# Layer 1: the products of a turned g with wphi issued one unit later, behind the next unit's turn

## The chip, the core and the metric

The kernel runs on one core of one Trainium2 chip. The metric is device time in microseconds of one execution; times are the median of several runs. TensorE (PE) does matmuls and transposes, VectorE (DVE), ScalarE (ACT) and GpSimd (POOL) do elementwise work, and SyncE (SP) issues nearly all DMAs.

## The reference, cut to what matters

A decaying causal attention over 4 batches, 8 heads and 576 positions is followed by a dense layer with a gated activation and by a soft mixture of 8 experts with 4 slots each:

```python
x = attention(q, k, v, f)                       # 2304 tokens x 512
h = x @ w_in                                    # 512 -> 2048
g = h * (1.0 / (1.0 + np.exp(-1.702 * h)))
x2 = g @ w_out                                  # 2048 -> 512
logits = x2 @ phi                               # 512 -> 32 slots
d = softmax(logits, axis=0); slot_in = d.T @ x2
slot_out[e] = np.maximum(slot_in[e] @ w1[e], 0.0) @ w2[e]
out = softmax(logits, axis=1) @ slot_out
```

Here `attention` and `softmax` stand for the reference's own lines, which are unchanged by what follows.

## The kernel before, in words

**What layer 1 computes.** The kernel never forms x2. It folds w_out and phi into one matrix, `wphi = w_out @ phi` (`fold_phi`, lines 240 to 257), so that the logits are `g @ wphi`, and it sums the slots' inputs in the space of g before it goes through w_out once at the end.

**How the work is tiled.** The 2304 tokens are 18 blocks of 128, taken two at a time: 9 chunks c = 0 to 8. A chunk has 8 units (t, fg): block t of two, quarter fg of the 2048 columns. `moe_steps` (lines 765 to 799) makes a unit: twelve fp16 matmuls into one PSUM bank `hp` (lines 775 to 777, four values of k times three products of high and low parts), then ScalarE's tanh (line 788) and VectorE's multiply (line 789) into `g`. The unit is put into the deque `turns`.

**The turn.** `turn(c, t, fg)` (line 731) is called at the end of a later unit; one unit as a rule stays in the deque. TensorE transposes g's four 128x128 pieces into a bank `gT` (line 744, f32), ScalarE copies the bank to `gt` in SBUF (line 751), and TensorE multiplies the four pieces by wphi into `p4` (line 753; the profile calls it p, and shows two records for each of the four f32 matmuls). The four products land in four groups of 32 partitions.

**What follows the last product of a chunk.** When all units of a chunk have been turned, `turn` runs off what is left of the steps of the chunk before and starts `slot_steps` (line 815): VectorE scales p4 into `l4` (line 820), TensorE sums it to logits `lg` in both orientations (lines 828 and 831), VectorE and ScalarE take running maximum and exponentials (lines 841 to 862), TensorE transposes the weights (`d`, line 871) and adds g up by slot (`sp`, line 896), and VectorE merges that into `spart` (line 903). These steps are a generator: each yield of `moe_steps` moves it by one. In the last chunk the two blocks have their own `p4` and their own slot steps.

**Attention beside it.** `attn_items` gives attention's pieces a place and a cost, and the main loop emits as many of them at each yield as a cumulative cost allows. Attention's last transposes of x (line 656) end in the seventh or eighth chunk. Then its pool is closed, and the loads of the expert weights (`load_e`, lines 1026, 1028 and 1031; 256 KB each, 127 of them) go through the SP queue into a ring of tiles: first new ones in the space that attention leaves, then `xt`, `g`, `w`, `gt` and other tiles as these come free. After layer 1 the experts' matmuls (lines 1147, 1169 and 1182) consume them.

**What sets the order.** The program is traced in the order of these calls, and when it is built a scheduler with a simulated timeline puts each engine's instructions in an order: on TensorE, work that the simulation holds ready can pass work that was traced earlier. `tc.issue_after(ins)` ties TensorE instructions of a block to places behind `ins`; no wait on a semaphore comes of it. On the chip each engine takes its instructions in that fixed order.

**Buffers that matter here.** PSUM: `sc` three banks, `mm` three (hp, gT, d, sp), `pv` one, `mi` one. `p4` and `lg` share the single `mi` bank. SBUF: `gt` has three buffers (`N_GT`), shared with the fold's transposed w_out in the first chunks; `g` has seven, of which a chunk takes four.

Of the kernel before, what the change touches and what calls it, by code (L numbers as in the profile page):

```python
# [30 lines left out]
def attention_moe_softmoe(ctx, tc, q, k, v, f, w_in, w_out, phi, w1, w2, out):  # L31
# [17 lines left out]
    NCH = NBLK // 2  # L49
# [11 lines left out]
    def ps_sc(name):  # L61
        return ps.tile([128, 512], F32, tag="sc", name=name, bufs=3)

    def ps_mm(name):
        return ps.tile([128, 512], F32, tag="mm", name=name, bufs=3)
# [4 lines left out]
    def ps_mi(name):  # L70
        return ps.tile([128, 512], F32, tag="mi", name=name, bufs=1)
# [646 lines left out]

    G = {}
    P4 = {}  # L720
    last_turn, last_hp = [None], [None]
    turns, turned, slot, sums = deque(), {}, [iter(())], {}
    N_UNIT = 2 * FG
# [2 lines left out]
    def units(c):  # L726
        if c == 0:
            return [(t, fg) for fg in range(FG) for t in range(2)]
        return [(t, fg) for t in range(2) for fg in range(FG)]

    def turn(c, t, fg):


        one = c == NCH - 1
        first = units(c)[0] if not one else (t, 0)
        if (t, fg) == first:
            P4[c, t if one else 0] = ps_mi("p4")
        p4 = P4[c, t if one else 0][:, 0 if one else 128 * t:][:, 0:128]
        g = G[c, t, fg]
        pt = pt2 = ps_mm("gT")  # L740
        if (c, t, fg) == (NCH - 1, 1, FG - 1):
            pt2 = ps_sc("gT")
        for a in range(4):
            last_turn[0] = nc.tensor.transpose((pt if a < 2 else pt2)[:, a * 128:(a + 1) * 128], g[:, a * 128:(a + 1) * 128], ident)  # L744
        gt = mp.tile([128, 512], F32, tag="gt", name="gt", bufs=N_GT)
        if (c, t, fg) == (NCH - 1, 1, FG - 1):
            nc.scalar.copy(out=gt[:, halves[0]], in_=pt[:, halves[0]])
            nc.vector.tensor_copy(gt[:, halves[1]], pt2[:, halves[1]])
            warm(2)
        else:  # L750
            nc.scalar.copy(out=gt, in_=pt)  # L751
        for a in range(4):
            nc.tensor.matmul(  # L753
                p4[NS * a:NS * (a + 1)], lhsT=wphi[:, 4 * fg + a, :], rhs=gt[:, a * 128:(a + 1) * 128],
                start=((t, fg) == first), stop=(fg == FG - 1), skip_group_check=True,
            )
        turned[c, t] = turned.get((c, t), 0) + 1
        ts = (t,) if one else (0, 1)
        if all(turned.get((c, i), 0) == FG for i in ts):
            for _ in slot[0]:  # L760
                pass
            slot[0] = slot_steps(c, ts)
            next(slot[0])

    def moe_steps(c):
        xt = XT[c]
        for u, (t, fg) in enumerate(units(c)):
# [5 lines left out]
            for kk in range(KD):  # L773
                with tc.issue_after(last_turn[0].ins) if final and kk == KD - 1 else nullcontext():
                    nc.tensor.matmul(hp, lhsT=xt[:, 0, kk, ts], rhs=win(0, fg, kk), start=(kk == 0), stop=False)  # L775
                    nc.tensor.matmul(hp, lhsT=xt[:, 0, kk, ts], rhs=win(1, fg, kk), start=False, stop=False)  # L776
                    last_hp[0] = nc.tensor.matmul(  # L777
                        hp, lhsT=xt[:, 1, kk, ts], rhs=win(0, fg, kk), start=False, stop=(kk == KD - 1)
                    )
                if kk == 1:  # L780
                    if final:
                        while turns:
                            turn(*turns.popleft())
                    yield
# [6 lines left out]
            for _ in range(min(3 if c < 2 else 2, len(turns) - 1)):  # L791
                if turns[0][2] >= folded[0]:
                    break
                turn(*turns.popleft())
# [7 lines left out]
    def warm(k):  # L802

        if not k:
            return
        if not idle:
            idle.append(ps_pv("z").rearrange("p (k n) -> p k n", k=4))
        for _ in range(k):
            tc.keep_in_program_order(
                nc.tensor.matmul(  # L810
                    idle[0], lhsT=ident16, rhs=ident16.unsqueeze(1).to_broadcast([128, 4, 128]), start=True, stop=True
                )
            )

    def slot_steps(c, ts=(0, 1)):
# [4 lines left out]
        nc.vector.tensor_scalar(  # L820
            out=l4, in0=P4.pop((c, ts[0]))[:, 0:128 * nt], scalar1=1.0 / (GS * WS), scalar2=None, op0=ALU.mult
        )
# [216 lines left out]
    if True:  # L1039
# [63 lines left out]
        while turns:  # L1103
            turn(*turns.popleft())
# [72 lines left out]
        for p, (c0, c1) in enumerate(PARTS):  # L1177
# [13 lines left out]
            p4 = (ps_mm if 1 else ps_mi)("p4")[:, 0:w]  # L1191
# [70 lines left out]
```

## Time and profile before

| | |
|---|---|
| median of 3 runs | 575.36 us (575.34 to 577.53) |
| the profiled execution | 572.58 us |
| its span, first to last instruction | 570.9 us |
| TensorE busy | 510.8 us, 89% of the span |
| VectorE, ScalarE, GpSimd busy | 353.3, 309.6, 69.0 us |
| mean granted TensorE clock | 0.97 |
| line 744, transposes of g (288) | 44.5 us, 278 ns each |
| line 751, copies of gT (71) | 40.8 us, 582 ns each |
| line 753, products with wphi (576 records) | 31.1 us, 286 ns each |
| lines 775 to 777, hp (864) | 332.3 us |

All rows are of the one profiled execution, on core 0. Times are microseconds from the start of the span. A row of the timeline gives the start, the duration, engine, source line, operation, and the tiles written and read; xN means that N like instructions were merged. A bracket at its end is the time that the engine stood idle before it and the instruction that ended the wait. Matmuls are pipelined, so the records of neighbours overlap and the distance of their starts says what one costs. A row of waits gives the total, the number of waits and the longest. DMA share is the mean busy share of the 16 DMA engines; their records can overlap, so it can come out above 1.

### The profile page before, as it was taken

To read this page: it belongs to the slowest core of one execution; us is meant where nothing else is said; L and a number is where in the kernel's file an instruction comes from. 1 tells how busy PE (TensorE), PEld (TensorE's weight loads), DVE (VectorE), ACT (ScalarE), POOL (GpSimd) and SP (SyncE) were. 2 spreads that over 40 slices of the span, in tenths; PEclk is the share of its full clock that TensorE was granted. 3 is DMA by queue.
4 is the path that set the end of the run, shared out by engine and by line. 5 is a ranking of instruction groups with operands and counts; after the bars stand their busy time and mean duration, and the time that the engine had idled before them with its cause. 6 is when DMAs were issued, how large, how long until landed. Compare 5 with 4: busy or idle time off the path is not lost.

```text
span 570.9 us, 13573 instructions
## 1 busy us (share of the span) xinstructions
PE 510.8 (89%) x5355; PEld 328.1 (57%) x5355; DVE 353.3 (62%) x934; ACT 309.6 (54%) x596; POOL 69.0 (12%) x120
## 2 busy tenths in 40 slices
PE   4476999999899989989999998988999999999991
PEld 4364877777666556655665664655566554454441
DVE  8978969476755676757685766867565323343032
ACT  5767686666765665646675565665565133312111
POOL 4766643220000000000000000000000000000000
PEclk9969799999999999999999998998999999999997
DMA  9997673978952869997648889986553189999998
GB/s 241 270 355 168 167 126 134 206 183 163 165 95 43 150 101 132 167 180 126 125 87 159 134 158 175 200 139 91 81 94 72 24 276 357 372 388 358 378 302 262
DMA packets 229823, 105.63 MB, mean 185 GB/s; under 512 B 202592, under 2 KB 211296, under 8 KB 229760
## 3 DMA queue, kind: packets, MB, share of 16 engines
q1 hardware_dynamic: 228528, 103.59, 77.9%
q10 hardware_dynamic: 1232, 1.18, 0.7%
q8 instruction: 42, 0.69, 0.5%
q14 instruction: 21, 0.17, 0.1%
HBM read 64.63 MB, written 4.72 MB: 121 GB/s over the span
## 4 chain that ended last, share of the span: by engine, by line
PE 62%; DMA 17%; DVE 9%; ACT 5%; issue 3%; SPq 2%; POOL 0%; DVEq 0%; ACTq 0%; POOLq 0%
PE hp L775 9%; PE hp L777 8%; PE hp L776 8%; DMA ph<-pn 6%; PE gT L744 5%; DMA we<-in_moe_w_dram 4%; PE p L753 4%; PE pv L607 3%; PE sp L896 3%; DMA kf<-in_k_dram 2%; PE pv L612 2%; DMA qf<-in_q_dram 2%; PE scs L536 2%; PE scs L535 2%; DVE low L213 1%
## 5 line engine op out<-in xcount | busy, mean ns | idle before, releaser
L775 PE MATMUL hp<-w,xt 128*128 128x512 f16 x288 | 111.0, 385 | 0.8 <-DVE spart L903 0.8
L776 PE MATMUL hp<-w,xt 128*128 128x512 f16 x288 | 110.7, 384 | 0.0
L777 PE MATMUL hp<-w,xt 128*128 128x512 f16 x288 | 110.6, 384 | 0.0
L562 ACT ACTIVATE pf<-scs,mx 128x512 f32<-128x512 f32 (+3 forms) x108 | 58.3, 543 | 40.7 <-DVE mx L558 30.4
L788 ACT ACTIVATE g<-hp 128x512 f32<-128x512 f32 x72 | 42.6, 592 | 53.0 <-PE hp L777 52.9
L571 DVE SCALAR_TENSOR_TENSOR pn<-pf,pn 128x512 f16<-128x512 f32 (+2 forms) x78 | 51.0, 657 | 32.1 <-ACT pn L570 31.6
L789 DVE SCALAR_TENSOR_TENSOR g<-g,hp 128x512 f32<-128x512 f32 x72 | 49.2, 683 | 34.6 <-ACT g L788 34.4
L570 ACT ACTIVATE pn<-pf 128x512 f16<-128x512 f32 (+2 forms) x78 | 46.9, 604 | 23.4 <-DMA ph<-pn 22.3
L558 DVE CUSTOM_DVE_ANT_0 scs<-scs,zmq 128x256 f32<-128x256 f32 (+3 forms) x96 | 46.9, 497 | 11.8 <-PE scs L536 6.8
L612 PE MATMUL pv<-vv,ph 128*128 128x65 f16 (+2 forms) x360 | 46.7, 198 | 3.5 <-DMA ph<-pn 3.4
L751 ACT COPY gt<-gT 128x512 f32<-128x512 f32 x71 | 40.8, 582 | 14.3 <-PE gT L744 13.5
L777 PEld LDWEIGHTS <-xt 128*128 128x128 f16 x288 | 28.5, 99 | 34.7 <-issue 2.8
L613 PE MATMUL pv<-vv,ph 128*128 128x65 f16 (+2 forms) x360 | 46.1, 196 | 0.0
L614 PE MATMUL pv<-vv,ph 128*128 128x65 f16 (+2 forms) x360 | 45.4, 194 | 0.0
L744 PE MATMUL gT<-ident,g 128*128 128x128 f32 x288 | 44.5, 278 | 1.0 <-DVE g L789 1.0
L775 PEld LDWEIGHTS <-xt 128*128 128x128 f16 x288 | 29.0, 101 | 25.7 <-issue 3.5
L612 PEld LDWEIGHTS <-ph 128*128 128x128 f16 (+2 forms) x360 | 34.5, 101 | 14.6 <-issue 5.8
L776 PEld LDWEIGHTS <-xt 128*128 128x128 f16 x288 | 28.5, 99 | 24.0 <-issue 2.3
L744 PEld LDWEIGHTS gT<-ident,g 128*128 128x128 f32 x288 | 33.3, 142 | 14.2 <-issue 5.1
L535 PE MATMUL scs<-kab,qa 128*128 128x128 f16 x240 | 35.4, 219 | 4.4 <-ACT pf L562 2.5
L613 PEld LDWEIGHTS <-ph 128*128 128x128 f16 (+2 forms) x360 | 34.9, 103 | 2.7 <-issue 0.4
L614 PEld LDWEIGHTS <-ph 128*128 128x128 f16 (+2 forms) x360 | 35.0, 103 | 0.7 <-issue 0.6
(223 smaller groups left out, 1013.4 us busy)
## 6 DMA issues: line engine op xcount, KB each, us to landing
we<-in_moe_w_dram SPq DMA_DIRECT2D x127, 256.0 KB, 5.4
raw<-in_moe_w_in_dram SPq DMA_DIRECT2D x16, 512.0 KB, 7.6
raw<-in_moe_w_out_dram SPq DMA_DIRECT2D x16, 512.0 KB, 6.0
kf<-in_k_dram SPq DMA_DIRECT2D x13, 256.0 KB, 3.7
qf<-in_q_dram SPq DMA_DIRECT2D x13, 256.0 KB, 4.4
vf<-in_v_dram SPq DMA_DIRECT2D x12, 256.0 KB, 4.5
out_dram<-ob SPq DMA_DIRECT2D x12, 256.0 KB, 3.2
ph<-pn SPq DMA_TRANSPOSE x78, 3.3
```

Of the source, the lines that this page charges most:

```text
L558: nc.vector.tensor_tensor_reduce(out=o, in0=o, in1=mask, scale=-SC, scalar=3.0e38 if n == 128 else DG[r][1][:, u], op0=ALU.add, op1=ALU.mi ...
L562: nc.scalar.activation(out=pf[:, hh * nb:(hh + 1) * nb], in_=o, func=AF.Exp, bias=mx[:, hh:hh + 1], scale=-1.0)
L570: nc.scalar.activation(out=pn[:, 0, 0:w], in_=pf, func=AF.Copy, scale=PB)
L571: nc.vector.scalar_tensor_tensor(out=pn[:, 1, 0:w], in0=pf, scalar=PB, in1=pn[:, 0, 0:w], op0=ALU.mult, op1=ALU.subtract)
L612: nc.tensor.matmul(o, lhsT=ph[0:rr, 0, off:off + n], rhs=vh, start=(j == 0), stop=False)
L613: nc.tensor.matmul(o, lhsT=ph[0:rr, 0, off:off + n], rhs=vl, start=False, stop=False)
L614: nc.tensor.matmul(o, lhsT=ph[0:rr, 1, off:off + n], rhs=vh, start=False, stop=(j == i))
L744: last_turn[0] = nc.tensor.transpose((pt if a < 2 else pt2)[:, a * 128:(a + 1) * 128], g[:, a * 128:(a + 1) * 128], ident)
L775: nc.tensor.matmul(hp, lhsT=xt[:, 0, kk, ts], rhs=win(0, fg, kk), start=(kk == 0), stop=False)
L776: nc.tensor.matmul(hp, lhsT=xt[:, 0, kk, ts], rhs=win(1, fg, kk), start=False, stop=False)
L777: last_hp[0] = nc.tensor.matmul(hp, lhsT=xt[:, 1, kk, ts], rhs=win(0, fg, kk), start=False, stop=(kk == KD - 1))
L789: nc.vector.scalar_tensor_tensor(out=g, in0=g, scalar=1.0, in1=hp, op0=ALU.add, op1=ALU.mult)
```

## The change

`turn` keeps the transposes and the copy. The four products, with the allocation of `p4` and the start of the slot steps that follows the last of them, become a function of their own, `by_phi`. A turn first runs `by_phi` for the unit held from the turn before, inside `tc.issue_after` of its own last transpose, and then puts its own unit into `held`. In the last chunk a unit isn't held: its products are issued at once, as before. The start of `slot_steps` for a chunk thus comes in the first turn of the next chunk.

```diff
+    held = deque()
...
     def turn(c, t, fg):
-        one = c == NCH - 1
-        first = units(c)[0] if not one else (t, 0)
-        if (t, fg) == first:
-            P4[c, t if one else 0] = ps_mi("p4")
-        p4 = P4[c, t if one else 0][:, 0 if one else 128 * t:][:, 0:128]
         g = G[c, t, fg]
         pt = pt2 = ps_mm("gT")
...
             nc.scalar.copy(out=gt, in_=pt)
+        with tc.issue_after(last_turn[0].ins):
+            while held:
+                by_phi(*held.popleft())
+        held.append((c, t, fg, gt))
+        if c == NCH - 1:
+            by_phi(*held.popleft())
+
+    def by_phi(c, t, fg, gt):
+        one = c == NCH - 1
+        first = units(c)[0] if not one else (t, 0)
+        if (t, fg) == first:
+            P4[c, t if one else 0] = ps_mi("p4")
+        p4 = P4[c, t if one else 0][:, 0 if one else 128 * t:][:, 0:128]
         for a in range(4):
             nc.tensor.matmul(
                 p4[NS * a:NS * (a + 1)], lhsT=wphi[:, 4 * fg + a, :], rhs=gt[:, a * 128:(a + 1) * 128],
```

What stands behind the products in `turn` (the count of turned units and the start of `slot_steps`) stands behind them in `by_phi` as well.

## Rows read from the trace of the kernel before

**Rows 1.** Windows of core 0: engine busy us (instructions), granted clock, DMA share, GB/s.

```profile
165.00:457.00 292.00, 278.33 (x3085) 172.22 (x3086) 192.17 (x556) 169.40 (x340) 3.56 (x30) 0.99 0.70 120
...
457.00:550.00 93.00, 89.42 (x857) 43.44 (x855) 25.45 (x85) 22.89 (x47) 0.68 (x1) 1.00 1.01 356
```

**Rows 2.** Waits of PE in 165 to 457: us in total, times, longest.

```profile
PE p L753 <- ACT gt L751: 3.4, 4, 2.1
```

**Rows 3.** Timeline of PE: start, us, instruction, [idle before <-releaser].

```profile
113.84 0.43 PE L753 MATMUL p<-gt,wphi 128*32 128x128 f32 x8 [0.71 <-ACT gt L751]
...
334.69 0.43 PE L753 MATMUL p<-gt,wphi 128*32 128x128 f32 x8 [0.94 <-ACT gt L751]
...
335.84 0.60 PE L744 MATMUL gT<-ident,g 128*128 128x128 f32 x4
...
380.93 0.42 PE L753 MATMUL p<-gt,wphi 128*32 128x128 f32 x8 [2.12 <-ACT gt L751]
...
383.89 0.19 PE L612 MATMUL pv<-vv,ph 128*128 128x65 f16 x1
```

**Rows 4.** Timeline of ACT, same columns, 378 to 381.

```profile
378.40 0.63 ACT L302 ACTIVATE kbn<-kf 64x512 f16<-64x512 f32 x1 [2.56 <-DMA kf<-in_k_dram]
...
380.31 0.56 ACT L751 COPY gt<-gT 128x512 f32<-128x512 f32 x1
```

**Rows 5.** Timeline of DVE, same columns.

```profile
334.38 0.68 DVE L789 SCALAR_TENSOR_TENSOR g<-g,hp 128x512 f32<-128x512 f32 x1
...
381.35 0.41 DVE L626 TENSOR_TENSOR x<-pv,rd 128x256 f32<-128x256 f32 x1
```

**Rows 6.** Waits of the SP queue in 440 to 460.

```profile
SPq L1026 <- DVE x L626: 9.5, 1, 9.5
...
SPq L1026 <- PE xT L656: 3.9, 1, 3.9
```

**Rows 7.** Timeline of PE, 457 to 466.

```profile
457.42 0.38 PE L656 MATMUL xT<-ident,x 128*128 128x128 f32 x2
...
460.96 0.38 PE L777 MATMUL hp<-w,xt 128*128 128x512 f16 x1
...
461.18 0.60 PE L744 MATMUL gT<-ident,g 128*128 128x128 f32 x4
...
461.70 0.42 PE L753 MATMUL p<-gt,wphi 128*32 128x128 f32 x8
...
462.06 0.39 PE L775 MATMUL hp<-w,xt 128*128 128x512 f16 x1
...
464.45 0.38 PE L777 MATMUL hp<-w,xt 128*128 128x512 f16 x1
...
464.76 0.42 PE L753 MATMUL p<-gt,wphi 128*32 128x128 f32 x8
...
465.11 0.66 PE L744 MATMUL gT<-ident,g 128*128 128x128 f32 x4
...
465.61 0.38 PE L775 MATMUL hp<-w,xt 128*128 128x512 f16 x1
```

**Rows 8.** Chain that ended last, in order of time, after 515.

```profile
524.94 5.42 DMA we<-in_moe_w_dram
```

**Rows 9.** Timeline of PE: the first and the last of nine.

```profile
169.72 0.43 PE L753 MATMUL p<-gt,wphi 128*32 128x128 f32 x8
...
433.08 0.43 PE L753 MATMUL p<-gt,wphi 128*32 128x128 f32 x8
```

**Rows 10.** Timeline of PE, 478 to 485.

```profile
478.80 0.59 PE L828 MATMUL lg<-l,rsum 128*128 128x256 f32 x2
...
481.50 0.30 PE L871 MATMUL d<-ident,dT 32*128 32x32 f32 x2 [1.27 <-ACT dT L860]
...
484.43 0.64 PE L753 MATMUL p<-gt,wphi 128*32 128x128 f32 x16
```

**Rows 11.** Timeline of DVE, 464 to 512.

```profile
481.74 0.22 DVE L841 TENSOR_TENSOR ee<-lg,rm 128x64 f32<-128x64 f32 x1
```

## The prediction

> **What bounds the kernel now.** I first read the windows of two stretches [rows 1]. From 165 to 457 us, where attention and layer 1 run interleaved, TensorE is busy 278.33 of 292.00 us at a granted clock of 0.99 while the DMA share is 0.70: TensorE sets the pace, and it stands still for 292.00 - 278.33 = 13.7 us. After 457 the picture turns: the DMA share is 1.01 at 356 GB/s, because the expert weights stream in. The chain of waits ends in these loads [rows 8]. The first of them waited for the end of attention: the SP queue stood 9.5 us for the last x and 3.9 us for its transposes [rows 6], which came at 457.42 [rows 7]. So a microsecond that TensorE loses before 457 delays the weight stream and, with it, the end; a microsecond gained inside the stream, between 457 and 510, is worth little.
>
> Next I read TensorE's waits of the first stretch. The wait that the change addresses, products (p) for the copied transpose (gt), is 3.4 us in 4 instances [rows 2]. The timeline shows where [rows 3]: 0.94 us at 334.69, 2.12 us at 380.93, two small ones between 165 and 457 making up the rest, and 0.71 us at 113.84, ahead of that stretch. The largest one's cause stands on ScalarE: it waited 2.56 us for the DMA of a k row, and the gt copy stood behind that row's casts until 380.31 [rows 4].
>
> What the order of TensorE looks like now matters as much. The products don't follow their own transposes even today: in [rows 7] the p at 464.76 belongs to the unit whose transposes ran at 461.18, and stands just ahead of the next unit's transposes at 465.11, a whole unit late. The change mostly moves a group of products from just before the next turn to just behind it.
>
> **The change part by part.** No instruction is added or removed: each of 72 units keeps four transposes, one copy (two in the last unit), and eight product records (p x8, 0.43 us). No DMA is issued by what moves; SP and POOL are passed by nothing.
>
> The stalls. With products held one turn longer, gt has been copied long before. Bounds: nothing, if each stall returns at the next instruction; the full 3.4 us of [rows 2] plus the 0.71 us of [rows 3] at the other end. I follow the two large ones. Without the 0.94 us, TensorE would reach its next transposes at 335.84 - 0.94 = 334.90 [rows 3], and their g is ready at 334.38 + 0.68 = 335.06 [rows 5]: 0.16 us returns. Without the 2.12 us, twelve hp matmuls follow that need nothing of ScalarE's late work; the attention products behind them need the bank that x frees at 381.35 + 0.41 = 381.76 [rows 5], and would come at 383.89 - 2.12 = 381.77 [rows 3]: nothing returns. So I take 3.4 - 0.16 = 3.2 us, and leave out the 0.71 us because before 165 weight loads and conversions share the path.
>
> The order on TensorE. Where p runs directly ahead of the transposes, hp to hp takes from 464.45 to 465.61 = 1.16 us; where transposes run ahead of p, from 460.96 to 462.06 = 1.10 us [rows 7]. The difference, 0.06 us, is what a group saves when it changes sides. Nine groups before 457 stand directly ahead of a whole turn [rows 9]: 9 x 0.06 = 0.5 us. The other groups have other work between, and I take nothing for them. The Trainium skill's page TensorE: Matmul & The Clock Gate (Step-by-step: what each phase is for) speaks against this term: weight loads are pulled ahead of matmuls in flight, so a change of sides should cost and save nothing. By it the sum would be 3.2 us instead of 3.7; here the row decides, since p starts 464.76 - 464.45 = 0.31 us after the last hp and the transposes 461.18 - 460.96 = 0.22 us.
>
> The logits chain. The last products of a chunk now come behind the first turn of the next chunk, so the copy l, both lg matmuls, the softmax and the slot sums (sp) start one unit later. Their lengths stay; the next chunk's first products move by a unit too, so the distance between them is kept. I take nothing. Bounds: below nothing, one group of products (0.43 us) slips past 457.42 and out of the path; above, a wait of 1.27 us like the one in [rows 10] at each of the seven chunk ends before 457, 8.9 us.
>
> Buffers. gt has three, and a held one plus the one being filled makes two. The g tiles of chunk 7 are freed by their sp a unit later, and the weight loads for those slots wait for that; the stream is then already full [rows 1], so I take nothing. In the last chunk nothing is held, so the tail stays.
>
> Sum: 3.2 + 0.5 = 3.7 us less. The profiled execution took 572.58 us (span 570.9), giving 568.9; it lies 2.78 us under the median of 575.36. On the median: 575.4 - 3.7 = 571.7 us.
>
> **Rivals.** *The waits only move (575).* ScalarE was late at 380 because a DMA was late [rows 4], and everything queued behind that cast was late with it. If what runs in the place of the products needs exp, cast or g, TensorE stands one instruction further on. The Trainium skill's page PSUM — Partial Sum Buffer (Engine vs sequencer instructions) says as much: ScalarE's queue is strictly first in, first out. For it: 10.3 of the 13.7 us idle have other causes, and the build-time scheduler places the whole stretch anew. Against it: twelve independent matmuls follow the largest stall. Only the order's 0.5 us would be left: 574.9.
>
> *The single p/lg bank stalls TensorE (580).* p and lg share one PSUM buffer. The next chunk's first products need every reader of lg done: lg starts at 478.80 [rows 10] and its last DVE reader ends at 481.74 + 0.22 = 481.96 [rows 11], 3.16 us later. Today TensorE fills that time with hp, and the first products of the last chunk run at 484.43, two units together [rows 10]. If products tied to a turn stand at TensorE's head earlier than 3.16 us after lg, it stands still. At 1.27 us a chunk end, seven ends give 8.9 us: 575.4 - 3.7 + 8.9 = 580.6. Against it: turns are 465.11 - 461.18 = 3.93 us apart even without attention [rows 7], over 3.16, and the tie orders products behind the turn without forbidding other work between.
>
> *The end of attention moves further (568).* The last x transposes at 457.42 stand behind twelve hp matmuls, and the loads waited 3.9 us for them [rows 6]. A new order that puts them ahead would start the stream up to 3.9 us sooner on top: 571.7 - 3.9 = 567.8. Nothing in the change forces it.
>
> *It does little, because the products are late already* [rows 7]; that ends where the first rival does, and is counted with it.
>
> **How the numbers follow.** About 0.5%, 2.9 us, is what a measurement of this kernel can tell from no change. Forecast 571.7, own range 569.5 to 573.5: 0.42. Waits only move, or little changes, 573 to 577: 0.33. Bank stall, 580.6: 0.17. Attention's end, 567.8: 0.08. Faster than 572.5 takes the two fast cases without the slow end of the forecast, to which I give 0.04: 0.42 - 0.04 + 0.08 = 0.46. Slower than 578.2 is the bank stall, 0.17; within 0.5% remains 0.37. The range 567 to 579 reaches down to the moved end of attention and leaves out the bank stall beyond 579, some 0.15, and 0.03 below.
>
> **What would show it.** The wait of p for gt should be gone from TensorE's waits, or below 0.5 us. TensorE's idle time between 165 us and the last x transposes should fall from 13.7 to about 10.5, and the first weight load should follow the last x transposes, 3 to 4 us sooner. Each group of products should stand right behind a turn, with hp to hp at 1.10 us. If the idle time is unchanged and other waits (ph, qa, lg) have appeared, the first rival holds. If p waits for a reader of lg, or the wait of d for dT grows at the chunk ends, the bank does. I am wrong altogether if the weight stream starts sooner and the end doesn't follow.

## The result and the profile after

The changed kernel took 568.45 us in the median of six runs (563.65 to 571.55) beside 575.35 us (574.63 to 577.53, six runs) before: a ratio of 0.9852 [0.9809, 0.9896] as recorded, 1.5% faster; the two medians alone give 0.988. Two repeats against new runs of before gave 0.989 [0.9847, 0.9933] and 0.9845 [0.98, 0.9891]. The profiled execution took 571.55 us (span 569.8), the longest of its six; those of the repeats took 565.27 and 561.29 us, so where it matters I read all three.

The windows of the kernel after, split where its first weight load starts (454 instead of 457); columns as in [rows 1]:

```profile
165.00:454.00 289.00, 277.34 (x3066) 169.01 (x3066) 191.82 (x554) 168.59 (x340) 3.57 (x30) 0.99 0.73 122
454.00:550.00 96.00, 92.87 (x881) 44.18 (x883) 26.12 (x86) 22.18 (x47) 0.68 (x1) 1.00 0.99 348
```

TensorE stands still for 289.00 - 277.34 = 11.7 us where it was 13.7, and the stage ends 3 us sooner. For a measure that doesn't hang on where a stage ends, I use one fixed window, 165 to 440, in every kernel: before

```profile
165.00:440.00 275.00, 261.33 (x2915) 162.44 (x2916) 184.94 (x533) 164.38 (x329) 3.56 (x30) 0.99 0.74 126
```

and after

```profile
165.00:440.00 275.00, 263.34 (x2925) 160.30 (x2925) 185.83 (x533) 165.56 (x332) 3.57 (x30) 0.99 0.76 127
```

Idle there is 13.7 us before and 11.7 after; a second profile of before gives 14.3, the two repeats of after 10.0 and 8.4.

What TensorE waited for, kernel before, 165 to 457, beside the line of [rows 2]:

```profile
PE pv L612 <- DMA ph<-pn: 3.2, 2, 2.8
PE lg L828 <- DVE l L820: 2.3, 1, 2.3
PE scs L535 <- DMA qa<-qan: 1.9, 1, 1.9
...
PE hp L775 <- DVE spart L903: 0.8, 1, 0.8
PE d L871 <- ACT dT L860: 0.8, 1, 0.8
```

The same view of the kernel after, 165 to 454:

```profile
PE pv L612 <- DMA ph<-pn: 7.5, 7, 2.7
PE gT L740 <- DVE g L798: 1.3, 2, 0.8
PE hp L784 <- ACT gt L747: 1.0, 1, 1.0
PE lg L837 <- DVE l L829: 0.6, 1, 0.6
```

Two things happened, and only one was in my forecast. The wait of p for gt is gone, but 1.0 us came back as a wait of hp (for the copy gt; hp and gT share three banks), and the wait for ph, the DMA that brings attention's probabilities, rose from 3.2 to 7.5 us (6.1 and 5.1 in the repeats). The other: three waits of the chain at the chunk's end, lg for l, d for dT and hp for spart, 2.3 + 0.8 + 0.8 = 3.9 us before, are down to 0.6 us (0.2 and 0.7 in the repeats). I had these rows before me and put them under "other causes".

The largest of them shows how it goes. Before, on TensorE's timeline:

```profile
251.14 0.70 PE L828 MATMUL lg<-l,rsum 128*128 128x256 f32 x2 [2.33 <-DVE l L820]
```

and on VectorE's:

```profile
250.59 0.19 DVE L307 COPY kan<-cpart 128x24 f16<-128x24 f16 x1 [2.59 <-DMA kab<-kan]
250.67 0.42 DVE L820 TENSOR_SCALAR l<-p 128x256 f32<-128x256 f32 x1
```

VectorE stood 2.59 us in front of a copy for attention that waited for a DMA; l was behind it in the queue, and lg was at TensorE's head, waiting for l. The same place after, on TensorE

```profile
250.64 0.38 PE L786 MATMUL hp<-w,xt 128*128 128x512 f16 x1
...
251.66 0.70 PE L837 MATMUL lg<-l,rsum 128*128 128x256 f32 x2 [0.65 <-DVE l L829]
```

and on VectorE:

```profile
250.51 0.19 DVE L307 COPY kan<-cpart 128x24 f16<-128x24 f16 x1 [2.99 <-DMA kab<-kan]
...
251.19 0.42 DVE L829 TENSOR_SCALAR l<-p 128x256 f32<-128x256 f32 x1
```

The DMA is as late (2.99 us) and l comes even later, at 251.19; but TensorE has hp matmuls of the next unit to run, the last of them from 250.64 to 251.02, and lg waits 0.65 us. The delay stayed, the work in front of it grew.

The order from the last x transposes on (timeline of TensorE, after) answers to [rows 7]:

```profile
454.37 0.38 PE L656 MATMUL xT<-ident,x 128*128 128x128 f32 x2
454.68 1.92 PE L905 MATMUL sp<-g,dd 128*32 128x512 f32 x16
...
459.87 0.38 PE L786 MATMUL hp<-w,xt 128*128 128x512 f16 x1
460.08 0.60 PE L740 MATMUL gT<-ident,g 128*128 128x128 f32 x4
460.61 0.43 PE L762 MATMUL p<-gt,wphi 128*32 128x128 f32 x8
460.97 0.39 PE L784 MATMUL hp<-w,xt 128*128 128x512 f16 x1
```

Products stand behind the turn, 460.97 - 459.87 = 1.10 us from hp to hp, as forecast. And chunk 6's slot sums (sp, 1.92 us) now stand behind the last x transposes; before, they ran ahead of them:

```profile
450.26 1.92 PE L896 MATMUL sp<-g,dd 128*32 128x512 f32 x16
```

My bound for what could slip out of the path there was 0.43 us.

The SP queue's wait at the end of attention, as in [rows 6], kernel after:

```profile
SPq L1035 <- PE xT L656: 3.4, 1, 3.4
```

and its longest one from 495 to 515:

```profile
SPq L1037 <- PE sw L938: 5.2, 2, 4.8
```

The first is nearly what it was (3.9): the transposes still stand behind twelve hp matmuls. The second, 5.2 us in two waits, was 2.7 us in two before (495 to 520); while SP waits, the stream thins out. The window of 510 to 515, before:

```profile
510.00:515.00 5.00, 5.00 (x82) 2.54 (x70) 4.04 (x12) 0.41 (x2) 0.68 (x1) 1.00 1.03 362
```

and after:

```profile
510.00:515.00 5.00, 5.00 (x91) 3.32 (x94) 3.52 (x11) 1.23 (x2) 0.68 (x1) 1.00 0.49 157
```

From the first weight load (457.8 before, 454.8 after) to the end of the span it takes 570.9 - 457.8 = 113.1 us before and 569.8 - 454.8 = 115.0 after: some 2 us of the gain are given back there, 1.4 us in the means of two profiles before and three after.

### The profile page after: what moved, and what is told of

It reads as the page before. It is cut to its first block, busy times and chain, and to the rows that moved or that the text cites. A ratio compares the mean times of both kernels' runs of the same rounds, so it can differ in the third digit from the quotient of the medians.

```text
span 569.8 us, 13581 instructions
## 1 busy us (share of the span) xinstructions
PE 512.9 (90%) x5355; PEld 325.7 (57%) x5355; DVE 353.0 (62%) x934; ACT 308.1 (54%) x596; POOL 68.8 (12%) x120
## 5 line engine op out<-in xcount | busy, mean ns | idle before, releaser
L797 ACT ACTIVATE g<-hp 128x512 f32<-128x512 f32 x72 | 42.5, 590 | 47.6 <-PE hp L786 42.6
L612 PE MATMUL pv<-vv,ph 128*128 128x65 f16 (+2 forms) x360 | 45.8, 198 | 8.4 <-DMA ph<-pn 7.5
L558 DVE CUSTOM_DVE_ANT_0 scs<-scs,zmq 128x128 f32<-128x128 f32 (+3 forms) x96 | 46.8, 497 | 10.2 <-PE scs L536 5.5
L740 PE MATMUL gT<-ident,g 128*128 128x128 f32 x288 | 45.2, 279 | 1.7 <-DVE g L798 1.3
L612 PEld LDWEIGHTS <-ph 128*128 128x128 f16 (+2 forms) x360 | 34.3, 101 | 19.0 <-DMA ph<-pn 10.0
L613 PE MATMUL pv<-vv,ph 128*128 128x65 f16 (+2 forms) x360 | 45.0, 195 | 0.0
L614 PE MATMUL pv<-vv,ph 128*128 128x65 f16 (+2 forms) x360 | 44.6, 194 | 0.0
L613 PEld LDWEIGHTS <-ph 128*128 128x128 f16 (+2 forms) x360 | 34.5, 102 | 2.2 <-issue 0.4
L569 POOL MEMSET pn<- 128x128 f16 x12 | 2.5, 206 | 272.3 <-DMA ph<-pn 268.7
```

What stands on the lines that cost most here:

```text
L558: nc.vector.tensor_tensor_reduce(out=o, in0=o, in1=mask, scale=-SC, scalar=3.0e38 if n == 128 else DG[r][1][:, u], op0=ALU.add, op1=ALU.mi ...
L612: nc.tensor.matmul(o, lhsT=ph[0:rr, 0, off:off + n], rhs=vh, start=(j == 0), stop=False)
L613: nc.tensor.matmul(o, lhsT=ph[0:rr, 0, off:off + n], rhs=vl, start=False, stop=False)
L614: nc.tensor.matmul(o, lhsT=ph[0:rr, 1, off:off + n], rhs=vh, start=False, stop=(j == i))
```

## The experiments

All kernels compute the same outputs. The theories: **A**, the removed stalls of p (the lag of the products) bring the gain; **B**, the later start of the chain at the chunk's end (l, lg, softmax, d, sp) brings it, because a late VectorE or ScalarE then finds TensorE busy; **C**, the sums of chunk 6 leaving the path before the first load bring it (1.85 us); **D**, the distance between dT and d alone; **R**, any other order of the attention pieces can do it, since the build places the whole stretch anew.

The table gives the ratio to the kernel before, the time of the profiled execution, TensorE's idle time in 165 to 440 in it (275.00 less its busy time), and its waits of lg and d together in that window. The profiled execution isn't always a typical one: those of e1, e2 and e6 were the slowest of their ten, that of e14 was the fastest of its twelve.

| kernel | ratio [95%] | profiled, us | idle, us | lg + d, us |
|---|---|---|---|---|
| before; again | 1 | 572.58; 575.07 | 13.7; 14.3 | 3.1; 3.3 |
| after | 0.9852 [0.9809, 0.9896] | 571.55 | 11.7 | 0.6 |
| a1_again | 0.989 [0.9847, 0.9933] | 565.27 | 10.0 | 0.2 |
| a3_after_third | 0.9845 [0.98, 0.9891] | 561.29 | 8.4 | 0.7 |
| e1_no_tie | 0.9947 [0.9918, 0.9975] | 571.87 | 12.1 | 0.5 |
| e2_no_chunk_lag | 1.0011 [0.9978, 1.0044] | 576.87 | 16.4 | 2.0 |
| e3_chunk_lag_only | 0.9865 [0.9804, 0.9926] | 561.66 | 9.0 | 0 |
| e3_repeat | 0.9859 [0.9808, 0.9909] | 563.28 | 9.1 | 0.3 |
| e4_chunk6_only | 1.0043 [1.0014, 1.0072] | 572.97 | 13.5 | 3.2 |
| e5_not_chunk6 | 0.9849 [0.9814, 0.9885] | 561.32 | 9.6 | 0 |
| e6_sums_later | 1.0096 [1.0061, 1.0131] | 580.22 | 14.9 | 4.2 |
| e7_d_later | 0.9864 [0.9819, 0.9909] | 563.54 | 8.9 | 0 |
| e8_chain_later | 0.984 [0.9793, 0.9887] | 562.07 | 9.4 | 0 |
| e9_two_later | 0.9899 [0.9848, 0.995] | 568.75 | 13.5 | 0.8 |
| e10_d_half_unit | 0.9799 [0.9766, 0.9832] | 559.99 | 9.4 | 0.8 |
| e11_d_two_units | 0.9813 [0.9783, 0.9844] | 561.12 | 11.7 | 0 |
| e12_after_d_back | 0.9868 [0.9819, 0.9916] | 563.41 | 10.5 | 3.6 |
| e13_order_cv110 | 0.999 [0.9958, 1.0022] | 571.55 | 12.8 | 2.8 |
| e14_order_cv92 | 0.9999 [0.9956, 1.0042] | 566.8 | 10.6 | 2.4 |

**The parts of the change, one by one.** The tie taken off (from after):

```diff
-        with tc.issue_after(last_turn[0].ins):
+        with nullcontext():
```

> The changed kernel without the tie: products are traced one turn later, but nothing holds them behind the turn on TensorE. Theory A and B: the lag does the work, 0.985 to 0.990, as the change. Rival C (the tie fixes an order that the build-time scheduler would not choose, and that order is what is won): 0.997 to 1.003, with p again ahead of gT.

0.9947, between the two ranges expected: the held products are then free to run earlier, and half of the gain (beside a1_again, measured with it) to two thirds (beside the first measurement) goes. The tie is part of what works, and not by way of the chain's place. A step's place on TensorE can be told by the units of hp (12 matmuls each) that ran ahead of it, counted in the traces: d stands behind 20, 28, 36, 44, 52 and 60 units at the ends of chunks 1 to 6, in after and in e1 alike, where it stood behind 19, 27, 35, 43, 51 and 59 before; lg stands within a third of a unit of its places in after, and lg and d wait as little (0.5 us).

The lag of the products kept, that of the chunk's end taken back:

```diff
-        if c == NCH - 1:
+        if c == NCH - 1 or (t, fg) == units(c)[-1]:
```

> The changed kernel with the last unit of each chunk issued at once: ordinary products still come one turn later, but each chunk's logits and slot sums start where they did before. Theory A: as the change, 0.985 to 0.990. Theory B: the 1.85 us of chunk 6's slot sums stand ahead of attention's last transposes again, so 0.003 of the gain is lost, 0.988 to 0.993. If the slot chain's lag is all there is: 1.000.

1.0011: nothing is left of the gain, though the wait that the change addresses is nearly gone. TensorE's waits, 165 to 440:

```profile
PE pv L612 <- DMA ph<-pn: 8.8, 7, 2.3
PE pv L612 <- DVE x L626: 2.0, 4, 0.8
PE d L880 <- ACT dT L869: 2.0, 2, 1.7
PE gT L740 <- ACT pf L562: 1.4, 1, 1.4
...
PE p L762 <- ACT gt L747: 0.6, 1, 0.6
```

p's wait fell from 3.4 to 0.6 us; waits for ph, x and pf (attention's probabilities, output and exponentials) and for dT took its place. A, as the cause of the gain, falls.

The opposite, only the last unit of a chunk (and the first of the next, which must come behind it in the same bank) held:

```diff
-        if c == NCH - 1:
+        if c == NCH - 1 or (t, fg) not in (units(c)[0], units(c)[-1]):
```

> Only the first and the last unit of each chunk are held one turn, the six between go at once as before: the slot chain starts one unit later, ordinary products don't. Theory A: the waits for gt come back, 0.998 to 1.002. Theory B: 0.3% to 0.4% from the slot sums alone, 0.996. If the slot chain's lag is all there is: 0.985.

> The kernel with only the chunk-end units held once more, beside its two halves. Both theories: 0.986, as in its first runs; the profile shows how far the start of the weight stream moves from one execution to the next.

0.9865 and 0.9859: the whole gain, with p still waiting 1.7 and 1.9 us for gt. Holding the other six of a chunk's eight units adds nothing that these ratios show.

**Which chunk's end.** Held at the end of chunk 6 alone, and everywhere but there:

```diff
+        if (c, t, fg) not in ((NCH - 3, *units(NCH - 3)[-1]), (NCH - 2, *units(NCH - 2)[0])):
```

> Only the last unit of chunk 6 and the first of chunk 7 are held; all other products and slot chains as in the kernel before. Theory H1 (what is won is chunk 6's slot sums and a group of products moving behind attention's last transposes, 1.85 + 0.36 = 2.2 us): 0.996, all of the gain that there is. Theory H2 (what is won is TensorE's idle time at every chunk end, where it waits for l, dT and spart: 2.3 + 0.8 + 0.8 us in the kernel before): 0.999 to 1.001.

> The complement: the units at all chunk ends are held but at that between chunks 6 and 7. Theory H1: 1.000, and chunk 6's slot sums stand ahead of attention's last transposes. Theory H2: 0.990 to 0.993, and TensorE's waits for l, dT and spart are below 1 us in sum.

1.0043 and 0.9849. C falls: moving chunk 6's sums past the last x transposes is worth nothing by itself, and the gain is complete without it. What e5 holds besides are the ends of chunks 0 to 5, beside attention, and that of chunk 7, under the weight stream, which was not tried by itself.

**The chain alone, in the kernel before.** Products stay where they were. Two yields (one unit) ahead of d; then two ahead of sp instead:

```diff
+        if not end:
+            for _ in range(2):
+                yield
         pd = ps_mm("d")
```

> The kernel before with two more yields ahead of the transposes d of chunks 0 to 7: d and the slot sums come one unit later, the logits and all products stay. Theory S (what is won is slack between steps of the chunk-end chain that TensorE waits for): the waits of d for dT are gone, 0.8 us before 445 us, those for l, 2.3 us, stay: 0.996 to 0.999. Theory T (what is won is that the chunk's last products and its logits come later, next to the following turn): 0.999 to 1.003. If d's slack is all there is: 0.985.

> The kernel before with two more yields ahead of the slot sums of chunks 0 to 7: sp and the merge into spart come one unit later, while the logits, the softmax and all products stay where they are. Theory H1: 0.997 (1.85 us of slot sums leave the path). Theory H2: 0.999 to 1.003, since the waits for l and dT stay.

0.9864 with d later, 1.0096 with only the sums later. Where in the chain the slack stands matters: in the latter d still waits 4.2 us. In e7 lg stands within half a unit of its places before, and yet its wait of 2.3 us is gone too, where the expectation for d's wait alone was 0.996 to 0.999. Half a unit ahead of d, and two units for chunks 1 to 6:

> The kernel before with one more yield, half a unit, ahead of the transposes d. Theory D (d stands right behind the exponentials that it needs, and whatever is queued behind it on TensorE waits with it; what is won is the distance): part of the gain or all of it, 0.986 to 0.996, and no wait of d for dT. Theory R (each of these kernels drew another build-time order, and the faster ones were lucky): anywhere between 0.985 and 1.010, with waits that don't follow the distance.

> The kernel before with d two units later in chunks 1 to 6 and one unit later in chunks 0, 7 and 8. Theory D: no more than with one unit, 0.984 to 0.990, since d already stands clear of dT there. Theory R: anywhere between 0.985 and 1.010.

One yield, 0.9799 [0.9766, 0.9832], 562.01 us, has the lowest ratio of this study; the change's three measurements are 0.9845 to 0.989, with intervals that reach into its own. More distance brings no more (0.9813). Its waits, 165 to 440:

```profile
PE pv L612 <- DVE x L626: 2.6, 1, 2.6
PE pv L612 <- DMA ph<-pn: 2.4, 5, 1.1
PE sp L899 <- DVE dd L876: 1.4, 1, 1.4
PE p L753 <- ACT gt L751: 1.0, 2, 0.8
PE d L874 <- ACT dT L860: 0.8, 1, 0.8
```

The wait of lg is gone here too, although only d was moved on purpose: in this order lg stands in the middle of a turn's transposes.

**The chain from its start, by another way.** Products at once, but the slot steps traced from the next chunk's first turn on (a deque `due` emptied beside `held`, and the first unit of each chunk held); then a lag of two turns at the chunk's end:

```diff
+            while due:
+                begin(*due.popleft())
...
+                due.append((c, ts))
```

> The chunk's last products are issued at once as in the kernel before, but its slot chain (l, lg and what follows) starts in the next chunk's first turn, and only the next chunk's first unit is held, since its products need the bank that lg gives back. Theory S: 0.985 to 0.988, all of the gain without moving the last products. Theory T: half of it or less, 0.993 to 1.000.

> The chunk's last unit and the next chunk's first are held two turns, the second one turn; the other products go at once. Theory S: as much as with one turn, 0.984 to 0.988, since a wait that is gone can't be won twice. If the gain were an accident of one build-time order: anywhere between 0.985 and 1.010.

0.984 and 0.9899. In e8, though, the order that the build made doesn't start the chain later on TensorE: lg stands behind 19, 26.5, 34, 42.25, 51 and 58 units of hp at the ends of chunks 1 to 6 (before: 19, 26, 34, 42.5, 51 and 58), and d one unit later than before, as in after. So e8 says again what e7 says: d later is enough, with the products at once. A second turn (e9) adds nothing.

**Is it d's distance?** From after, the yields ahead of d cut by two:

```diff
-            for _ in range(3):
+            for _ in range(1):
                 yield
```

> The changed kernel with two of the three yields ahead of d taken out, which puts d and the slot sums where they were traced before the change; products and logits stay a turn later. Theory D: the change's gain is gone, 0.998 to 1.008, and TensorE waits for dT again, 1 us or more before attention's end. If the later products and logits were what is won: 0.985 to 0.989 as the change.

0.9868. The wait comes back, the time doesn't:

```profile
PE pv L612 <- DMA ph<-pn: 5.1, 6, 2.1
PE d L880 <- ACT dT L869: 3.6, 3, 2.0
```

Here d stands behind 19, 27, 35, 43, 51 and 59 units, as before the change. So D is enough in the kernel before (e7, e10), but the gain of the change doesn't need it: with the products and logits later, 3.6 us of waits of d cost nothing that the comparison shows.

**Repeats.** The kernel after twice more, and before once (a profile for comparison).

> The changed kernel once more, for a second profile and a narrower interval. Theory A (the products' lag removes TensorE's waits for gt and nothing else): ratio 0.994, the weight stream starts at about 454.8 as in the first profile, and the rest of the time is the same in every profile. Theory B (the lag also moves chunk 6's slot sums, 1.85 us, out of the way of attention's end, and what is won there is partly given back when the loads meet TensorE's sw): ratio 0.985, and where a profile is shorter than the first one's 569.8 us it is so after 505 us, in a smaller wait of the SP queue for sw.

> The changed kernel a third time, beside the three above on one chip: 0.985 to 0.989.

> The kernel before once more, for a second profile: 1.000. If the waits at chunk ends belong to the order and not to one execution, lg for l, d for dT and hp for spart again wait about 4 us in sum before attention's end, and the weight stream starts 5 to 10 us later than in the profiles of the variants with the chain moved.

The second profile of before has the same waits at the same instructions (lg 2.5, qa 1.8, d 0.8, spart 0.7, gt 4.1 us): they belong to the order that the build gave, not to one execution.

**Any other order?** The kernel before with one of the planner's costs changed, so that attention pieces fill other gaps nearly everywhere while the chain stays:

```diff
-        CE, CV, CM, CR, CP, CX = (800, 100, 300, 100, 500, 430)
+        CE, CV, CM, CR, CP, CX = (800, 110, 300, 100, 500, 430)
```

> The kernel before with one number of the planner changed: the cost that it charges to a head's weighted sum of values (CV) is 110 in place of 100. Nothing of the expert chain is moved on purpose (the products stand right behind the turn, the logits chain where it stood); what changes is which attention piece fills which gap, almost everywhere in the attention stage. If the gain belongs to slack of the chain at the chunk's end, this kernel has none more than before: ratio 0.995 to 1.005, TensorE idle between the turn of unit (1, 4) and the first weight load 12 to 15 us, waits of lg and d together 2 us or more. If any other order of the fillings can bring such a gain, the ratio lies outside 0.995 to 1.005 on either side, and where it is below, TensorE idle is under 11.7 us although lg or d still wait.

> The same with CV at 92 in place of 100. Slack of the chain: ratio 0.995 to 1.005, TensorE idle 12 to 15 us in the same stretch, lg and d waiting 2 us or more together. Any order: outside 0.995 to 1.005 on either side, and where it is below, idle under 11.7 us with lg or d still waiting. Both kernels inside 0.5% speak for slack; one of them at 0.99 or below shows that no lag of the chain is needed for a gain of this size.

0.999 and 0.9999: no gain. In the first, TensorE waits for lg as before, and more for ph:

```profile
PE pv L612 <- DMA ph<-pn: 8.8, 6, 3.0
PE lg L828 <- DVE l L820: 2.8, 2, 1.8
PE p L753 <- ACT gt L751: 0.7, 2, 0.4
```

It also answers A once more: p waits 0.7 us instead of 3.4, at the same time. The second expectation fails for idle time: 10.6 us were seen in an execution of 566.8 us, the fastest of its twelve (median 575.17), so one profile's idle time doesn't stand for the kernel. Two other orders don't exclude R. What the traces do show is a pattern in d's place: it comes half a unit to two units later at the ends of most chunks in after, e3, e5, e7, e8, e10 and e11, at 0.980 to 0.989, and in e9, at 0.990; it stands where it stood before in e2, e6, e13 and e14, and in e4 but for chunk 6, at 0.999 to 1.010. Two kernels don't fit: e12, with d where it was, has the gain (0.987), and e1, with d as late as in after, has a third to half of it. So B is borne out as far as d's place goes; that the shorter waits of the chain are what brings the gain is not shown, and e1 speaks against them as the whole of it. For what is left over R stands, and no run excludes it.

## Why the prediction was right or wrong

The direction was right and 568.45 us lies in the range, but the gain came out at 575.35 - 568.45 = 6.9 us (8.5 us by the ratio) instead of 3.7, and from another place: the term that carried the forecast brought nothing, so the right direction was luck.

*The stalls* (3.2 us, the term that carried the sum): wrong. The wait of p went as described, and in the change 1.0 us returned as hp's wait for the copy. The rest moved to ph; e2, which has this part alone, is at 1.0011. The rival "the waits only move" was right for this part: ScalarE and the DMAs were late, and what ran in the place of the products needed them too. My argument followed two stalls through the order of before, but the build placed the stretch anew.

*The order on TensorE* (0.5 us): not seen. The page's rows by line, whole span, after, for the turn, the products and the sums:

```profile
L740 PE MATMUL gT<-ident,g 128*128 128x128 f32 x288 | 45.2, 279 | 1.7 <-DVE g L798 1.3 <-DVE wphi L255 0.3
L762 PE MATMUL p<-gt,wphi 128*32 128x128 f32 x576 | 32.3, 286 | 1.9 <-ACT gt L747 1.6 <-DVE dd L882 0.3
L905 PE MATMUL sp<-g,dd 128*32 128x512 f32 x136 | 16.6, 597 | 0.0
```

Transposes and products together rose by 45.2 + 32.3 - 44.5 - 31.1 = 1.9 us, where a fall was expected; 1.10 us from hp to hp holds only for a turn with nothing beside it. The sums fell by 18.9 - 16.6 = 2.3 us, because sixteen now run in one piece, where products stood between them before. The two nearly cancel.

*The logits chain* ("Their lengths stay ... I take nothing"): this is the step that failed. What was put at nothing is the whole gain: holding only the units at the chunks' ends gives 0.9865 and 0.9859 (e3), moving d alone 0.9864 (e7). The step looked at the lengths and at what could come to wait, and not at what the chain's steps already waited for: lg 2.3, d 0.8 and hp for spart 0.8 us. After the change these are 0.2 to 0.7 us in all. My bound for "below nothing" was 0.43 us; these rows alone would have made it 3.9. That the gain comes through these waits stays open (e1, e12).

*The account.* Means of two profiles before and three after, 165 to 440: idle falls from 14.0 to 10.0 us, 4.0 less. Chain waits fall by 3.4 (3.9, 4.0 to 0.6, 0.2, 0.7); waits for gt by 2.6 (3.4, 4.1 to 1.0, 1.2, 1.2) while those for ph rise by 2.9 (3.2, 3.5 to 7.5, 6.1, 5.1); 0.9 is left for the small ones. The mean of the profiled times falls by 573.8 - 566.0 = 7.8 us; beyond the idle time, one to three stretches at half clock fewer (below; 3.4 us of work on the means) and an earlier start (ScalarE begins the g of chunk 1's fifth unit between 164.4 and 169.8 us, some 2 us sooner on the means, but 5 us apart among executions of after alone) make it up, and the tail takes some 1.4 us back. So the idle time is about half of it.

*Buffers* (nothing): slightly wrong. The loads that wait for sw thin the stream between 510 and 515.

*The single p/lg bank*: no wait of p for a reader of lg stands among the lines of after between 165 and 454. The turns behind the last x transposes stay 463.57 - 460.08 = 3.49 us apart, over the 3.16 us for which the bank was held before. *The end of attention*: its transposes still stand behind twelve hp, as the 3.4 us show; this rival did not come in.

*Left open.* That a later place of d at the chunks' ends brings the gain to the kernel before is shown by e7, e10 and e11, each in the order that its build gave; by what way is not. In e1 the chain is as late as in after and waits as little, and half of the gain or more is missing; in e12 d waits 3.6 us again at no cost, and e10 gains more than the change with 0.8 us of d left. Every edit moves attention's pieces too: e7, e8 and e10 run one unit of hp fewer ahead of the first load than before and after do (so does e14, which gains nothing). Why the sums alone (e6) cost 1% was not followed further than its rows: d waits 4.2 us, and TensorE's clock is lower.

## What to carry to other kernels

When a step moves, list every wait of the steps that move with it, also those that the change isn't about: the wait that falls away may be theirs. On an engine that does its instructions in a fixed order, a short dependent chain across three engines should have independent work between each of its links on the busiest one; here half a unit of hp ahead of d was worth 2%, and more was worth no more, though not all of that can be traced to its wait. Removing a wait whose cause is a late DMA or another engine's queue gains nothing if what comes next needs the same: here 2.8 us of it went and the ratio was 1.0011 (e2). And when a scheduler makes the order, read from the trace where the moved step came to stand: in e8 the start of the chain, traced later, did not run later.

## What was not expected of the hardware

TensorE's granted clock fell to its lower level (0.50, 1.2 of 2.4 GHz) after some waits and not after others. The waits of before are 2.12 us for gt at 380.93 [rows 3] and 1.87 us for qa:

```profile
346.55 0.29 PE L535 MATMUL scs<-kab,qa 128*128 128x128 f16 x2 [1.87 <-DMA qa<-qan]
```

The windows behind them:

```profile
347.00:349.00 2.00, 1.99 (x46) 1.63 (x39) 1.61 (x9) 1.06 (x3) 0.00 (x0) 0.92 1.11 227
349.00:350.00 1.00, 1.00 (x13) 0.69 (x11) 0.18 (x1) 0.71 (x2) 0.00 (x0) 0.50 0.65 130
...
382.00:384.00 2.00, 2.00 (x14) 0.94 (x13) 1.63 (x3) 1.59 (x4) 0.00 (x0) 1.00 0.44 69
```

The shorter one was followed by half clock from 348.7 to 352.1, the longer by full clock. The stretches of before last 3.4 us each, one in its second profile 6.8; at half clock that loses an estimated 1.7 and 3.4 us of work. Between 170 and 440 the two profiles of before lose 3.4 and 6.8 us in this way, and each of those of after 1.7 us, as in this window of after:

```profile
384.00:386.00 2.00, 2.00 (x6) 0.76 (x5) 0.40 (x2) 0.53 (x1) 0.00 (x0) 0.50 0.76 147
```

The chain's waits are among those that were followed by half clock: one stretch of before (396.5 to 399.9) begins 0.5 us behind the wait of d at 396.04, and the long one of its second profile (250.6 to 257.4) at the end of lg's wait of 2.5 us, as in this window:

```profile
253.00:254.00 1.00, 1.00 (x3) 0.30 (x2) 0.84 (x6) 0.42 (x2) 0.07 (x2) 0.50 0.78 179
```

In the first profile of before and in e14 the same wait of lg was followed by full clock. So what follows a wait can cost as much as the wait, but the row of the wait doesn't tell whether it does. Nor had I expected executions of one kernel to differ as much as those of after, 561.29 to 571.55 us in the three profiled ones, of three sessions, and 563.65 to 571.55 us in one session, more than the gain itself; a single run would not have told these kernels apart.
